# A one-core decode kernel: its first load cut into 16 and 112 rows, and the last output chunks put into other column groups

## The chip, the cores and the metric

The kernel runs on 1 core of one Trainium2 chip. The metric is the device time of one execution in microseconds. Three runs of the kernel before gave 746.25, 746.13 and 745.9, the median is 746.13.

## The reference

One token `x` of 576 features is normalised, and two branches are added to it.

```python
xn = _layernorm(x, axis=-1)
return x + _A_ref(xn, ...) + _B_ref(xn, ...)
# A: q = xn @ wq, 32 heads of 128; scores over 8192 cached keys, scale 128 ** -0.5
#    p = softmax(scores); o = p @ v_cache; out = o.reshape(1, 1, 4096) @ wo
# B: gate = xn @ W_gate, up = xn @ W_up (4608 wide); h = gate * (gate > 0) * up; out = h @ W_down
```

Everything is float32. For each of 32 heads the cache holds 8192 x 128 keys and as many values, 4.2 MB each; with the weights the program reads 319 MB, each byte once, and writes 576 numbers.

## The kernel before

**Loads.** Three buffers in SBUF, `slot0` to `slot2`, of 128 rows (partitions) x 16384 floats, are filled in turn by DMAs that SyncE (SP) issues in one written order. The helper `load` (its DMA is line 159) issues one DMA for one buffer, or for a part of its columns. The first three need no wait: `wq` into slot 0 (128 rows of 64 KB, the query weights), `wqt` into slot 1 (the rest of the query weights and a first part of gate and up weights), `wg` into slot 2 (more of them). Then come 32 loads `kv[n]`, each with the values of head n - 1 in the first half of the columns and the keys of head n in the second (the first one has gate and up weights in place of values), `vw`, and nine loads of `wod`, the rows of `wo` and `W_down` in one order, 576 columns for each chunk of 128 rows. A load waits until its buffer has been read, so up to two wait in the DMA queue behind the one that moves. The DMAs of an issuing engine go through one queue, and 16 DMA engines work on it.

**Work.** Layer norm is done by VectorE (DVE) and ScalarE (ACT) on one row while `wq` is on its way. TensorE (PE) then computes `q` with 36 matmuls into the bank `bq`, of which the first waits for `wq` and the thirty-third for `wqt`. Each head's keys are multiplied with the broadcast query on DVE (line 287) and summed (line 292), ACT takes the exponentials (line 306), and PE sums the values with them (helper `values`; all plain matmuls have line 216).

**End.** There are 68 output chunks, f = 0 to 67: 32 heads of `wo` and 36 parts of `W_down`. Each adds one row of 576 numbers as two matmuls of 288 columns (j = 0, 1). A float32 matmul is two instructions in the trace, so a chunk is four MATMULs. Output row r selects the column group of PE in which a matmul runs. Even chunks go to rows 0 and 32 of the bank `acc` (called here the lower column groups), odd ones to rows 64 and 96 of the bank `ac2` (the upper ones); the last `LAST` = 4 chunks, 64 to 67, all go to the lower groups. When chunk 63 is done (mark "odd"), DVE adds the odd chunks' sum to `x2`, in which `x` already lies in rows 64 and 96 (line 412, mark "y"); PE adds the result to `acc` with two matmuls (four MATMULs) that pick these rows with columns of the identity. These stand in PE's order after chunk 65 and ahead of chunks 66 and 67:

```python
if f == end - 2:
    for j in range(2):
        mm(("y",) if j == 0 else (), None, acc[32 * j:32 * j + 1, :N2],
           ident[:, 64 + 32 * j:65 + 32 * j], x2, False, False)
```

After chunk 67, DVE and ACT each copy one half of the result out of `acc` (lines 413 and 414), and SP writes it out (line 182). `OUT` sets how the chunks are grouped into loads: 9 of them come with `vw`, then one load of 28, loads of 9, 7, 5, 4 and 3, and one load each for chunks 65, 66 and 67. Their matmuls wait for "o" of their own load.

Each engine runs its list in the written order. Waits are on semaphores; each DMA here has one, which reaches its full count when all 16 DMA engines are done.

Of the kernel before, what the change touches and what calls it, by code (L numbers as in the profile page):

```python
# [9 lines left out]
P = 128  # L10
# [13 lines left out]

OUT = ((9,), (28,), (9, 7, 5, 4, 3), (1, 1, 1))

LAST = 4

UNITS = (28, 32, 16, 5)

# [6 lines left out]
class Program:  # L37
# [19 lines left out]
    def add(self, engine, f, waits=(), mark=None, on=None, by=1):  # L57
        to = None
        if mark is not None:
            to = on or engine  # L60
            self.sem(to)
            self.counts[to] += by
            assert mark not in self.marks, mark
            self.marks[mark] = (to, self.counts[to])
        self.lists[engine].append((f, tuple(waits), to, by))
# [41 lines left out]
def build(nc, x, kv, vw, wq, wqt, wg, wod, out):  # L107
    pr = Program(nc)
    add = pr.add

    def sb(name, shape):
        return nc.alloc_sbuf_tensor(name, list(shape), F32).ap()

    def bank(name):
        return nc.alloc_psum_tensor(name, [P, 512], F32).ap()

    slots = [sb(f"slot{i}", [P, W]) for i in range(3)]
# [13 lines left out]
    xz = sb("xz", [P, 4, 37])  # L131
# [15 lines left out]
    bq, bb, bm, bo, bt, acc, ac2, bx = [bank(f"bank{i}") for i in range(8)]  # L147
# [9 lines left out]
    def load(name, k, src, waits, on, start=0):  # L157
        dst = slots[k % 3][:, start:start + src.shape[-1]]
        add("sync", lambda e: e.dma_start(dst, src), waits, name, on=on, by=16)  # L159

    def tile(n):
        return slots[(n + 3) % 3]

    load("wq", 0, wq, (), "dwq")
    load("g0", 1, wqt, (), "dg0")
    load("g1", 2, wg, (), "dg1")
    load(("t", 0), 3, kv[0], ("pq",), "dt0")
# [6 lines left out]
    f = OUT[0][0]  # L174
# [40 lines left out]
    def mm(waits, mark, o, lhsT, rhs, start, stop):  # L215
        add("tensor", lambda e: e.matmul(o, lhsT, rhs, start=start, stop=stop), waits, mark)  # L216
# [5 lines left out]
    for k in range(36):  # L222
        if k < 32:
            r, a, j = k // 16, k // 4 % 4, k % 4
            mm(("wq", "xz") if k == 0 else (), None, bq[32 * j:32 * j + 32, :], xz[:, a, 5 - r:37 - r],
               slots[0][:, a * 4096 + (4 * r + j) * 512:][:, :512], k < 4, False)
        else:
            j = k - 32
            mm(("g0", "xt") if k == 32 else (), "pq" if k == 35 else None, bq[32 * j:32 * j + 32, :], xt[:, 5:37],
               slots[1][:, j * 512:(j + 1) * 512], False, True)  # L230
# [105 lines left out]
    for n in range(1, H):  # L336
        k, i = (n - 1) // G, (n - 1) % G
# [52 lines left out]
    f, end = 0, H + FC  # L390
# [3 lines left out]
    for k, loads in enumerate(OUT):  # L394
        t = tile(H)[:, SK + UNITS[3] * 512:] if k == 0 else slots[(H + 3 + k) % 3]
        i = 0
        for n in loads:
            for m in range(n):
                waits = (("o", f),) if m == 0 and k else ()
                waits += needs.get(f, ())  # L400
                odd = f % 2 and f < end - LAST
                for j in range(2):
                    r = 64 * odd + 32 * j
                    mark = {OUT[0][0] - 1: ("first", f), end - LAST - 1: "odd", end - 1: "even"}.get(f) if j else None
                    mm(waits if j == 0 else (), mark, (ac2 if odd else acc)[r:r + 1, :N2], order[f], t[:, i * D + j * N2:][:, :N2],
                       f < 2, f in (end - LAST - 1, end - 1))
                f += 1
                i += 1
                if f == end - 2:
                    for j in range(2):  # L410
                        mm(("y",) if j == 0 else (), None, acc[32 * j:32 * j + 1, :N2], ident[:, 64 + 32 * j:65 + 32 * j], x2, False, False)
    add("vector", lambda e: e.tensor_add(x2[64:P, :], ac2[64:P, :N2], x2[64:P, :]), ("odd", "x2"), "y")  # L412
# [62 lines left out]
```

## Time and profile before

| what | value |
|---|---|
| median of three runs | 746.13 us |
| the profiled execution | 745.72 us, of which 744.2 us lie between its first and last instruction (the span) |
| PE, DVE, ACT, POOL busy | 41%, 78%, 5%, 0% of the span |
| queue q1 (SP's loads) | 319.17 MB, 99.3% of the time of 16 DMA engines |
| mean granted TensorE clock | 0.661 of full speed |

The span leaves 1.5 us of the profiled execution outside. The profiled execution is 0.41 us below the median. Busy shares are means over the whole span; the start (no data yet) and the end (no data left to load) have other limits than the middle.

### The profile page before, as it was taken

Reading aid. Unit: us, or ns where it says so; the run is one execution under the profiler, and the core shown is the slowest. Engines: PE = TensorE matmul, PEld = TensorE weight load, DVE = VectorE, ACT = ScalarE, POOL = GpSimd, SP = SyncE. Lnnn points to the kernel's source line nnn. Section 1 sums busy time; section 2 is a strip of 40 time slices with the busy share of each in tenths; the row PEclk is TensorE's granted clock in tenths of the full one; section 3 lists DMA queues with packets and bytes.
Section 4 is the critical chain, followed back from the end, with each engine's and each line's share of the span. In section 5 each row is a group of like instructions: output and inputs, shape, how many; then the busy total and the mean of one; then the engine's idle time right before and its main releaser. Section 6 shows DMA issues by size and latency. Waiting matters only on the chain.

```text
span 744.2 us, 4062 instructions
## 1 busy us (share of the span) xinstructions
PE 302.0 (41%) x1752; PEld 87.4 (12%) x1752; DVE 577.2 (78%) x177; ACT 36.5 (5%) x114; POOL 2.1 (0%) x10
## 2 busy tenths in 40 slices
PE   1454413343253343352343344334324325334677
PEld 1111100010010010010010011001001001001122
DVE  2000189999989999989999998998998998999610
ACT  1000001010010010010000001001001000000000
POOL 1000000000000000000000000000000000000000
PEclk9967755767655565556556656655565565565789
DMA  9999999999999999999999999999999999999997
GB/s 395 451 420 426 445 451 402 440 451 405 444 447 413 444 437 444 416 440 444 412 440 447 412 440 444 412 447 437 437 423 440 444 412 437 451 409 438 432 414 319
DMA packets 6498, 319.30 MB, mean 429 GB/s; under 512 B 724, under 2 KB 726, under 8 KB 1240
## 3 DMA queue, kind: packets, MB, share of 16 engines
q1 hardware_dynamic: 6482, 319.17, 99.3%
q8 instruction: 6, 0.10, 0.1%
q14 instruction: 4, 0.03, 0.0%
q10 hardware_dynamic: 6, 0.00, 0.0%
HBM read 319.16 MB, written 0.00 MB: 429 GB/s over the span
## 4 chain that ended last, share of the span: by engine, by line
DMA 45%; DVE 22%; issue 20%; PE 11%; ACT 1%; SPq 0%; DVEq 0%; ACTq 0%
DMA slot<-in_kv 35%; DVE slot L287 12%; PE bank L216 11%; DVE s L292 9%; DMA slot<-in_wqt 5%; DMA slot<-in_wod 5%; ACT row L310 1%; ACT pzs L306 0%; DVE nb L296 0%; DVE mr L293 0%; SPq L159 0%; DVE os L300 0%; DVE row L413 0%; DVE rl L299 0%; DVEq L101 0%
## 5 line engine op out<-in xcount | busy, mean ns | idle before, releaser
L287 DVE TENSOR_TENSOR slot<-slot,bank 128x8192 f32<-128x8192 f32 x32 | 277.9, 8686 | 82.3 <-PE bank L216 65.8
L292 DVE TENSOR_REDUCE s<-slot 128x64 f32<-128x8192 f32 x32 | 277.6, 8676 | 0.0
L216 PE MATMUL bank<-slot,pzs 128*12 128x512 f32 x1024 | 184.7, 888 | 201.9 <-ACT pzs L306 201.9
L216 PEld LDWEIGHTS bank<-slot,pzs 128*12 128x12 f32 x1024 | 35.4, 123 | 332.5 <-issue 332.3
L216 PE MATMUL bank<-slot,xz 128*32 128x512 f32 x208 | 36.7, 732 | 32.1 <-DMA slot<-in_wq 12.8
L216 PE MATMUL bank<-ident,mr 128*128 128x128 f32 x64 | 17.6, 360 | 73.8 <-DVE mr L293 73.7
L216 PE MATMUL bank<-l,ones 128*128 128x3 f32 (+1 forms) x22 | 6.3, 354 | 98.2 <-ACT pzs L306 98.2
L306 ACT ACTIVATE pzs<-s,nb 128x64 f32<-128x64 f32 x32 | 11.1, 348 | 457.3 <-issue 419.4
L237 DVE TENSOR_SCALAR row<-bank 128x512 f32<-128x512 f32 x1 | 0.7, 692 | 33.8 <-PE bank L216 33.8
L216 PEld LDWEIGHTS bank<-ident,mr 128*128 128x128 f32 x64 | 10.7, 210 | 95.6 <-DVE mr L293 95.4
L412 DVE TENSOR_TENSOR x<-bank,x 64x288 f32<-64x288 f32 x1 | 0.5, 460 | 26.9 <-PE bank L216 26.9
L216 PEld LDWEIGHTS bank<-l,ones 128*128 128x128 f32 x22 | 5.3, 299 | 101.5 <-ACT pzs L306 100.7
L274 ACT ACTIVATE dq<-ident,qs 128x128 f32<-128x128 f32 x32 | 10.7, 392 | 130.7 <-PE bank L216 90.6
L216 PE MATMUL bank<-dq,ones 128*128 128x384 f32 (+1 forms) x24 | 15.3, 737 | 0.0
L216 PEld LDWEIGHTS bank<-slot,xz 128*32 128x32 f32 x208 | 8.5, 131 | 57.8 <-issue 23.6
L216 PE MATMUL bank<-sel,row 128*128 128x3 f32 (+1 forms) x88 | 11.6, 254 | 7.9 <-ACT row L310 7.9
L216 PE MATMUL bank<-slot,os 128*1 128x288 f32 x128 | 11.3, 500 | 4.7 <-DMA slot<-in_wod 4.7
L216 PEld LDWEIGHTS bank<-sel,row 128*128 128x128 f32 x88 | 10.6, 191 | 17.5 <-ACT row L310 17.5
L216 PE MATMUL bank<-slot,hh 128*1 128x288 f32 x144 | 11.2, 406 | 3.2 <-DMA slot<-in_wod 3.2
L216 PE MATMUL bank<-slot,xt 128*32 128x512 f32 x26 | 6.8, 1021 | 10.8 <-DMA slot<-in_wqt 10.8
L310 ACT COPY row<-bank 128x512 f32<-128x512 f32 x11 | 6.4, 585 | 77.2 <-PE bank L216 77.2
L296 DVE TENSOR_REDUCE nb<-bank 128x1 f32<-128x128 f32 x32 | 9.1, 284 | 0.6 <-PE bank L216 0.6
(52 smaller groups left out, 54.3 us busy)
## 6 DMA issues: line engine op xcount, KB each, us to landing
slot<-in_wod SPq DMA_DIRECT2D x1, 8064.0 KB, 39.3
slot<-in_vw SPq DMA_DIRECT2D x1, 7968.0 KB, 39.6
slot<-in_wod SPq DMA_DIRECT2D x1, 2592.0 KB, 25.9
slot<-in_wod SPq DMA_DIRECT2D x1, 2016.0 KB, 30.4
slot<-in_wod SPq DMA_DIRECT2D x1, 1440.0 KB, 33.3
slot<-in_wod SPq DMA_DIRECT2D x1, 1152.0 KB, 35.6
slot<-in_wod SPq DMA_DIRECT2D x1, 864.0 KB, 36.9
slot<-in_wod SPq DMA_DIRECT2D x3, 288.0 KB, 25.0
```

The lines of the kernel that those rows point to most:

```text
L216: add("tensor", lambda e: e.matmul(o, lhsT, rhs, start=start, stop=stop), waits, mark)
L237: add("vector", lambda e: e.tensor_scalar_mul(row, bq, SCALE), ("pq", "n7"), "qr")
L274: add("scalar", lambda e, m=m, h=h: e.activation(dq[:, m, :], ident, AF.Copy, scale=qs[:, h:h + 1]), (free,) if m == 0 else (), ("dq", k) ...
L287: add("vector", lambda e: e.tensor_mul(k3, k3, qb[:, m, None, :].to_broadcast([P, C, DH])), waits, ("mul", h))
L292: add("vector", lambda e: e.reduce_sum(s, k3, axis=AX.X), (("mul", h),), ("sum", h))
L296: add("vector", lambda e: e.tensor_reduce(nb[h % 2], pm, axis=AX.X, op=ALU.max, negate=True), (("pm", h),), ("nb", h))
L306: add("scalar", lambda e: e.activation(pz[:, i, :, 4 * G - 4:4 * G], s2[h % 2].rearrange("p (c b) -> p c b", b=4), AF.Exp, bias=nb[h % 2], ...
L310: add("scalar", lambda e: e.copy(row, bo), (("V", h),) + ((("ot", k - 1),) if k else ("pqt",)), ("oc", k), on="oc", by=STEP)
L412: add("vector", lambda e: e.tensor_add(x2[64:P, :], ac2[64:P, :N2], x2[64:P, :]), ("odd", "x2"), "y")
```

## The change

It has two parts that don't touch each other. The load of `wq` becomes two DMAs on the same queue, rows 0 to 15 and rows 16 to 127, each with its own semaphore; the first matmul of `q` waits for both. `LAST` becomes 2, so chunk 64 stays in the lower and chunk 65 goes to the upper column groups; the mark "odd" moves from chunk 63 to chunk 65, and the four MATMULs that add `x2` move from after chunk 65 to after chunk 66.

```diff
-LAST = 4
+LAST = 2
...
-    load("wq", 0, wq, (), "dwq")
+
+    add("sync", lambda e: e.dma_start(slots[0][:16, :], wq[:16]), (), "wq0", on="dwq0", by=16)
+    add("sync", lambda e: e.dma_start(slots[0][16:P, :], wq[16:]), (), "wq", on="dwq", by=16)
     load("g0", 1, wqt, (), "dg0")
...
-            mm(("wq", "xz") if k == 0 else (), None, bq[32 * j:32 * j + 32, :], xz[:, a, 5 - r:37 - r],
+            mm(("wq0", "wq", "xz") if k == 0 else (), None, bq[32 * j:32 * j + 32, :], xz[:, a, 5 - r:37 - r],
...
-                if f == end - 2:
+                if f == end - 1:
```

## The prediction

> **What bounds the kernel now.** I read the page first, for which engine has no idle time, then the DMA queue over the middle of the run, then the first and the last microseconds instruction by instruction.
>
> ```profile
> PE 302.0 (41%) x1752; PEld 87.4 (12%) x1752; DVE 577.2 (78%) x177; ACT 36.5 (5%) x114; POOL 2.1 (0%) x10
> DMA  9999999999999999999999999999999999999997
> q1 hardware_dynamic: 6482, 319.17, 99.3%
> DMA 45%; DVE 22%; issue 20%; PE 11%; ACT 1%; SPq 0%; DVEq 0%; ACTq 0%
> ```
>
> No engine is near its limit: DVE is busy 78%, PE 41%. The queue of loads is: the packets of q1 fill 99.3% of the time of 16 DMA engines, and every slice of the span but the last is full. The chain of waits names DMA, DVE and PE, but a chain also passes through work that merely runs beside the loads. The view by windows settles it for the middle (columns: window, its length, busy time of PE, PEld, DVE, ACT, POOL, clock, DMA share, GB/s):
>
> ```profile
> 20.00:730.00 710.00, 289.99 (x1624) 81.81 (x1628) 571.48 (x160) 32.48 (x108) 0.00 (x0) 0.64 1.00 432
> ```
>
> From 20 to 730 us the DMA share is 1.00. So a microsecond that the queue loses or gains anywhere ahead of 730 us moves the end by one, unless a load is issued too late. The issues and their times to landing (us, last number) say that this has slack:
>
> ```profile
> slot<-in_wq SPq DMA_DIRECT2D x1, 21.7
> slot<-in_wqt SPq DMA_DIRECT2D x1, 40.6
> slot<-in_wg SPq DMA_DIRECT2D x1, 60.8
> slot<-in_kv SPq DMA_DIRECT2D x32, 39.3
> ```
>
> A `kv` load is issued 39.3 us before it lands, while one load takes about 19.3 us (next fence), so there is a whole load queued ahead of it.
>
> **The change part by part: the start.** The timeline of the first stretch:
>
> ```profile
> 0.73 0.52 ACTq L194 DMA_DIRECT2D row<-in_x  x1
> 0.74 0.40 SPq L159 DMA_DIRECT2D slot<-in_wq  x1
> 1.20 0.42 SPq L159 DMA_DIRECT2D slot<-in_wqt  x1
> 1.66 0.42 SPq L159 DMA_DIRECT2D slot<-in_wg  x1
> 22.53 8.53 PE L216 MATMUL bank<-slot,xz 128*32 128x512 f32 x64 [12.77 <-DMA slot<-in_wq]
> 41.85 1.94 PE L216 MATMUL bank<-slot,xt 128*32 128x512 f32 x8 [10.79 <-DMA slot<-in_wqt]
> 43.85 28.06 SPq L159 DMA_DIRECT2D slot<-in_kv  x3
> ```
>
> Three loads are issued within 1.4 us, yet their readers start at 22.53 and 41.85 us, 19.3 us apart: the queue serves whole loads one after the other. That is the point on which I rest: 16 rows in a DMA of their own are moved first, with nothing of the other 112 rows beside them to fill engines that they leave slow.
>
> How the 16 DMA engines begin, by slices of 0.05 us from 1 to 3 us, and by windows (same columns as above):
>
> ```profile
> GB/s 0 0 0 0 0 0 0 0 0 0 0 0 0 46 0 5243 1311 3932 2621 2621 0 0 0 0 2621 1311 0 0 1311 0 0 0 0 0 0 0 0 0 0 0
> q1 hardware_dynamic: 16, 1.05, 152.1%
> 1.70:2.50 0.80, 0.00 (x0) 0.00 (x0) 0.44 (x2) 0.12 (x1) 0.27 (x3) 1.00 3.80 1311
> 2.50:4.70 2.20, 0.00 (x0) 0.00 (x0) 0.96 (x3) 2.17 (x4) 0.00 (x0) 1.00 0.00 0
> 4.70:5.30 0.60, 0.00 (x0) 0.00 (x0) 0.00 (x0) 0.60 (x1) 0.00 (x0) 1.00 4.03 1748
> ```
>
> Bytes are counted where a packet starts. 16 packets, 1.05 MB, start between 1.75 and 2.45 us: 64 KB each, one row for each engine. None starts from 2.50 to 4.70, the next 16 do so by 5.30. So a load is 8 turns of one row per engine, 19.3 / 8 = 2.4 us a turn, 27 GB/s per engine.
>
> *The earlier start.* The first DMA now has 16 rows to be set up instead of 128. The nearest row is the one-row load of `x`: issued at 0.73, its 2.2 KB packet is the 46 in the slice from 1.65, 0.92 us later. From the issue at 0.74 that would be 1.66, against first packets from 1.75 to 2.45 now. So between 0.1 and 0.8 us are to be gained on an engine; a few of the 16 start late, most by 2.0, so I take -0.3. Below it -0.8; above it +0.3, for one more completion per engine and a set-up that gains nothing.
>
> *The second DMA.* SP issues one more, some 0.46 us by the step from 0.74 to 1.20. `wq`'s rest then goes at 1.20, `wqt` at 1.66, `wg` at 2.12. The first rows keep the engines busy to about 4.7 us, so nothing runs dry; the next issue on SP is `kv[0]` at 43.85, which waits for PE. Cost 0. POOL's and ACT's queues are not passed. The extra wait ("wq0") stands ahead of the first matmul of `q`; all of PE is behind it, but it was already waiting 12.77 us for `wq`, which lands later than `wq0`. Cost 0 while that holds.
>
> *What 16 neighbouring rows cost.* In every load of this trace the 16 engines work on all 128 rows. No row shows them on rows 0 to 15 only. Fast end: they take one turn as now, 2.4 us, cost 0. Slow end: each set of rows takes bytes no faster than it does in a full load, where rows 0 to 15 take theirs in the whole 19.3 us; cost 19.3 - 2.4 = +16.9. Neither row is nearer, since both are of full loads: one shows what an engine can send, the other what these rows took. I take the middle, (2.4 + 19.3) / 2 = 10.9 us, hence +8.4, and keep 0 and +16.9 for the range. Cover: none, by the DMA share of 1.00.
>
> The Trainium skill, "SBUF — State Buffer", section "Door 1: The DMA port swizzle", says that a DMA's rate goes by how many of 16 ports its partitions reach, that partitions 0 to 15 reach four, and that 1 MiB to them was measured at 104 GB/s. By it this DMA would take an estimated 1.05 MB / 104 GB/s = 10.1 us instead of 2.4, and the sum would be 753.5. No row here shows such a DMA.
>
> *The 112 rows.* Seven turns per engine. Fast end: 7 x 2.4 = 16.9 us, as in a full load, cost 0. Slow end: two engines meet at each turn and halve, cost +16.9. The nearest row is the full load, which differs by 16 rows of 128: I take 0.
>
> **The change: the end.** PE's and DVE's timeline, and the three single-chunk loads (65, 66, 67) with their least, median and longest time to landing:
>
> ```profile
> 739.38 1.62 PE L216 MATMUL bank<-slot,hh 128*1 128x288 f32 x16 [0.98 <-DMA slot<-in_wod]
> 740.11 0.46 DVE L412 TENSOR_TENSOR x<-bank,x 64x288 f32<-64x288 f32 x1 [26.93 <-PE bank L216]
> 740.62 0.30 PEld L216 LDWEIGHTS bank<-x,ident 128*1 128x1 f32 x4 [0.19 <-DVE x L412]
> 740.83 0.66 PE L216 MATMUL bank<-x,ident 128*1 128x288 f32 x4
> 741.31 1.14 PE L216 MATMUL bank<-slot,hh 128*1 128x288 f32 x8
> 742.50 0.45 DVE L413 COPY row<-bank 1x288 f32<-1x288 f32 x1 [1.93 <-PE bank L216]
> L216 PE MATMUL bank<-x,ident x4: 406/406/406, 740.8 to 741.1; 128*1 128x288 f32 x4
> L159 SPq DMA_DIRECT2D slot<-in_wod x3: 328/418/430, 715.3 to 716.2; - x3
> DMA to landing us min/median/max: 24.7/25.0/25.3
> ```
>
> A MATMUL of 288 columns lasts 0.41 us (406 ns). The 8 of chunks 66 and 67, all in the lower groups, take 1.14: (1.14 - 0.41) / 3 = 0.24 us from step to step, two steps a chunk. The 16 of chunks 62 to 65 take 1.62, (1.62 - 0.41) / 0.24 = 5 intervals, six steps: 62 and 63 share two, 64 and 65 take two each. Chunks 65, 66 and 67 land at 715.3 + 24.7 = 740.0, about 740.7, and 716.2 + 25.3 = 741.5.
>
> Before, from 739.38 on: 62/63, 64, 65, y, 66, 67, twelve steps without a gap, 739.38 + 11 x 0.243 + 0.41 = 742.46. DVE's add (740.11 to 740.57) lay wholly under 64 and 65. After: 62/63 at 739.38 and 739.62; 64 at 739.86 and 740.10; 65, released at 740.0, beside 64's second step at 740.10 and then at 740.34. It ends at 740.75. DVE starts 0.08 later, as it did after chunk 63 (739.62 + 0.41 = 740.03, start 740.11): 740.83 to 741.29. The cover for it is now chunk 66 alone (landed 740.7, steps 740.78 and 741.02, over by 741.27). The matmuls of y, queued ahead of chunk 67, wait to 741.34 and 741.58; chunk 67 follows at 741.82 and 742.07, end 742.47. Chunk 67 landed at 741.5 and waits for y in both kernels. So two steps saved in the column groups (-0.49) come back as a wait for DVE: 0.0. If 65 lands one step earlier against PE it is -0.24, one later +0.24.
>
> **Sum**, on the profiled execution: 745.72 - 0.3 + 8.4 + 0 + 0.0 = 753.8. The median lies 0.41 higher, so 754.2.
>
> **The rivals.**
>
> *Not slower: the 16 rows take one turn.* Then the split does what it says and the stream begins earlier: 746.13 - 0.3 + 0.0 = 745.8, with -0.8 and -0.24 at best 745.1, with +0.3 and +0.24 at worst 746.7. For it: an engine sends 27 GB/s to a row today, and its share is the same with 16 rows. Against it: nothing shows that neighbouring rows accept 16 engines at once. It decides from 1.2 us on: if the 16 rows take less than 2.4 + 0.3 + 1.5 = 4.2 us, the result is within 0.2% (1.5 us, about what a measurement of this kernel can tell from no change).
>
> *The 112 rows are uneven as well.* Rows 16 to 127 no longer start where the engines' shares of a full load start. At half of the slow end, +8.4, on top of the forecast: 762.6. For it: one engine late is enough, since a load's semaphore waits for all. Against it: 112 is seven full turns of 16.
>
> *Faster by more than 1.5 us.* The best ends together are -0.8 - 0.24 = -1.0, 745.1; so it needs something that no row shows.
>
> **How the numbers follow.** Forecast 45%; the uneven 112 rows 10%; not slower 42%; clearly faster 3%. I put the two sides close together, as the fence of the first packets leaves the 16 rows open between 2.4 and 19.3 us, and only 1.5 of those 16.9 us belong to "no change"; but the fast end is one plain case and the slow side a spread. Slower by over 0.2%: 45 + 10 = 55%; within: 42%; faster: 3%. The range goes from 745.1, the good end of the rival, to 763.0 (746.13 + 16.9), and leaves out parts of the last two. The forecast's own range is 749 to 763.
>
> **What would show it.** Slow 16 rows: few bytes start between 5 and 12 us, q's first matmul moves from 22.53 to about 30.6 us, the `wqt` readers from 41.85 to about 49.9, and all later steps of 19.3 us stay. One turn: q's first matmul is at about 22.2. Uneven 112 rows: the first matmul later than 33. At the end: the `x2` add (now L414) starts 0.8 us after chunk 65 lands in place of beside its matmuls, PE has a gap of some 0.07 us between chunk 66 and y, and the span from PE's start on chunks 62 to 64 to the copies stays 3.1 us. The prediction is wrong if the first load lands as early as before, or if the end moves by more than 0.3 us by itself.

## The result and the profile after

The changed kernel takes 767.36 us (median of 6 runs, 766.39 to 768.51) against 746.23 for the kernel before (6 runs, 745.9 to 747.5): 1.0284 times as long, 95% interval 1.027 to 1.0297. It is slower by 21.1 us; the forecast was 754.2, slower by 8, with a range up to 763.0.

The page of the changed kernel, the lines that answer to those shown of before, and the rate by slices:

```profile
PE 300.0 (39%) x1752; PEld 88.3 (12%) x1752; DVE 576.8 (75%) x177; ACT 36.5 (5%) x114; POOL 2.1 (0%) x10
DMA  9999999999999999999999999999999999999997
GB/s 165 267 380 432 438 438 407 433 438 438 421 438 431 435 438 435 428 425 438 438 438 431 428 438 431 431 438 435 431 425 438 438 438 425 431 438 433 430 412 304
q1 hardware_dynamic: 6498, 319.17, 99.2%
DVE 48%; DMA 40%; PE 7%; issue 4%; another core or an unknown queue 1%; ACT 0%; SPq 0%; DVEq 0%; ACTq 0%
```

The busy times are the same within some 2 us, and the DMA share hardly moved: 99.2% and a row of nines, in a run that lost 21 us in its loads. The share counts the time that packets took, and a packet that crawls counts as busy. The loss is in the line below it: 165, 267 and 380 GB/s in the first three slices (19.1 us each), 407 and more after that, but for the last slice (304; 319 before). A DMA share has to be read beside its GB/s. The shares of the chain moved (DVE from 22% to 48%, issue from 20% to 4%, DMA from 45% to 40%) although DVE's busy time did not change (577.2 and 576.8 us): the chain passes through work that runs beside the loads.

The first stretch of the changed kernel, then its windows from 3 to 9.5 and from 12 to 43 us, and the same windows of the kernel before (columns: window, length, PE busy, clock, DMA share, GB/s):

```profile
0.74 0.39 SPq L165 DMA_DIRECT2D slot<-in_wq  x1
1.19 0.40 SPq L166 DMA_DIRECT2D slot<-in_wq  x1
1.64 0.42 SPq L159 DMA_DIRECT2D slot<-in_wqt  x1
44.50 9.23 PE L218 MATMUL bank<-slot,xz 128*32 128x512 f32 x64 [34.73 <-DMA slot<-in_wq]
63.75 1.94 PE L218 MATMUL bank<-slot,xt 128*32 128x512 f32 x8 [10.02 <-DMA slot<-in_wqt]
```
```profile
3.00:9.50 6.50, 2.45 (x12) 1.00 0.00 0
12.00:43.00 31.00, 0.00 (x0) 1.00 0.91 233
```
```profile
3.00:9.50 6.50, 2.45 (x12) 1.00 0.75 323
12.00:43.00 31.00, 9.68 (x72) 0.88 1.01 438
```

q's first matmul starts at 44.50 us in place of 22.53, 22.0 us later; the readers of `wqt` at 63.75 in place of 41.85, 21.9 later and again 19.3 us after the first load. So the whole loss is in the first load, and it is there by 44.5 us. It has two parts. From 3 to 9.5 us no new packet starts at all: the first 16 are still under way (a window counts a packet, its time and its bytes, where it starts, so its DMA share of 0.00 does not mean idle engines). Then the 112 rows move at 233 GB/s, about half the 438 of before. The first DMA (line 165) took 12.5 us from issue to landing, the second (line 166) 43.2:

```profile
DMA to landing us min/median/max: 12.5/12.5/12.5
```
```profile
DMA to landing us min/median/max: 43.2/43.2/43.2
```

They land at 0.74 + 12.5 = 13.2 and 1.19 + 43.2 = 44.4 us. So the 112 rows had 31.2 us, where seven turns of 2.4 are 16.9.

The end of the changed kernel, then the last part of the chain of work that ended last:

```profile
760.95 2.09 PE L218 MATMUL bank<-slot,hh 128*1 128x288 f32 x20 [0.96 <-DMA slot<-in_wod]
762.35 0.46 DVE L414 TENSOR_TENSOR x<-bank,x 64x288 f32<-64x288 f32 x1 [26.47 <-PE bank L218]
762.86 0.66 PE L218 MATMUL bank<-x,ident 128*1 128x288 f32 x4
763.35 0.66 PE L218 MATMUL bank<-slot,hh 128*1 128x288 f32 x4
764.05 0.45 DVE L415 COPY row<-bank 1x288 f32<-1x288 f32 x1 [1.24 <-PE bank L218]
```
```profile
738.41 23.93 DMA slot<-in_wod
762.34 0.04 issue
762.38 1.65 PE bank L218 x12
```

From PE's start on chunks 62 to 64 to the copies it is 764.05 - 760.95 = 3.10 us; before, 742.50 - 739.38 = 3.12. The steps saved in the column groups came back as a wait for the load of chunk 66. The chain passes through its landing at 762.34, and the 12 MATMULs behind it are chunk 66, y and chunk 67. Chunk 66 starts at 762.38, its two steps of 0.24 us are over at 762.86, and y starts there without a gap. DVE was done a little earlier (line 414 ends at 762.81).

### The profile page after: what moved, and what is told of

Its sections match the earlier page's. It is cut to its first block, busy times and chain, and to the rows that moved or that the text cites. A ratio compares the mean times of both kernels' runs of the same rounds, so it can differ in the third digit from the quotient of the medians.

```text
span 765.7 us, 4063 instructions
## 1 busy us (share of the span) xinstructions
PE 300.0 (39%) x1752; PEld 88.3 (12%) x1752; DVE 576.8 (75%) x177; ACT 36.5 (5%) x114; POOL 2.1 (0%) x10
## 3 DMA queue, kind: packets, MB, share of 16 engines
q1 hardware_dynamic: 6498, 319.17, 99.2%
## 4 chain that ended last, share of the span: by engine, by line
DVE 48%; DMA 40%; PE 7%; issue 4%; another core or an unknown queue 1%; ACT 0%; SPq 0%; DVEq 0%; ACTq 0%
DMA slot<-in_kv 26%; DVE slot L289 24%; DVE s L294 23%; PE bank L218 7%; DMA slot<-in_wq 6%; DMA slot<-in_vw 5%; DMA slot<-in_wod 3%; DVE mr L295 1%; DVE nb L298 1%; ACT row L312 0%; DVE os L302 0%; DVEq L101 0%; DVE rl L301 0%; ACT pzs L308 0%
```

## The experiments

Theory "rows": how fast the 16 DMA engines fill a buffer depends on which rows they are on together; a DMA whose rows don't lie evenly over all 128 goes at a part of the rate. Its rivals: a second DMA costs by itself; the number of rows costs (few, or no power of two); the end of the kernel has a part in the loss. ("The page on SBUF ports" in the expectations is the page of the Trainium skill that the prediction cites; a "group of rows" there is the rows behind one of its 16 ports.) Kernels with an interval were timed beside the kernel before. The others are one execution each; the kernel before gave 745.66 to 747.74 in these series, so single times are read to some 2 us.

**One part of the change at a time.**

```diff
 e1: -LAST = 2 / if f == end - 1      +LAST = 4 / if f == end - 2      (the changed kernel, with the end of before)
 e2: -LAST = 4 / if f == end - 2      +LAST = 2 / if f == end - 1      (the kernel before, with the new end)
```

> Only the split of the first load (16 and 112 rows); the end as before. If the split carries the loss: 767 to 768 us, q's first matmul at about 44.5 us in place of 22.5. If the end has a part in it: under 766.

> Only the end is changed (last two chunks in the lower column groups, the odd sum added ahead of the last chunk alone); the first load is whole. By the steps of the prediction: 746.2, within 0.3 us of before, PE's stretch from the chunks 62 to 64 to the copies 3.1 us. Rival: the end costs or gains more than 0.5 us.

The split alone: 766.8 us, a little under the 767 to 768 expected, ratio 1.027 (1.0255 to 1.0286), q's first matmul at 44.56. The end alone: 745.92 against 746.06, ratio 0.9996 (0.9987 to 1.0005). The end of e2:

```profile
739.55 2.08 PE L216 MATMUL bank<-slot,hh 128*1 128x288 f32 x20 [0.97 <-DMA slot<-in_wod]
740.96 0.46 DVE L412 TENSOR_TENSOR x<-bank,x 64x288 f32<-64x288 f32 x1 [27.69 <-PE bank L216]
741.47 0.65 PE L216 MATMUL bank<-x,ident 128*1 128x288 f32 x4
742.66 0.45 DVE L413 COPY row<-bank 1x288 f32<-1x288 f32 x1 [1.24 <-PE bank L216]
```

742.66 - 739.55 = 3.11. The split carries all of the loss within the noise, and the end is worth nothing in either direction.

**Is it the second DMA, the count, or the rows?** In e3 to e10 the first load is cut in other ways; all else is the kernel before. Each piece has its own semaphore, and q's first matmul waits for all.

```diff
-    load("wq", 0, wq, (), "dwq")
+    # e3: rows :64 and 64:            e4: all rows, columns :2048 and 2048:
+    # e5: rows 0::2 and 1::2          e6: rows i::8, i = 0 to 7
+    # e7: rows 16*i:16*i+16, i = 0 to 7   e8: rows :112 and 112:
+    # e9: rows :32 and 32:            e10: rows i::4, i = 0 to 3
+    add("sync", lambda e: e.dma_start(slots[0][:64, :], wq[:64]), (), "wq0", on="dwq0", by=16)   # e3
+    add("sync", lambda e: e.dma_start(slots[0][64:P, :], wq[64:]), (), "wq1", on="dwq1", by=16)
```

> The first load in two DMAs of 64 rows each (0 to 63, 64 to 127); the end as before. Theory rows (each group of rows takes only its own share of the rate; by the page on SBUF ports 64 neighbouring rows reach half of 16 ports): each half takes twice its time, the first load lands some 19 us later, 765 us. Rival count (112 is no power of two, or is 7 rows an engine, and that is slow): no loss, 746. Rival two DMAs (the second one's set-up or completion costs): the same as with 16 and 112 rows, 767.

> The first load in two DMAs of all 128 rows, columns 0 to 2047 and 2048 to 16383; the end as before. Theory rows: no loss, 746 within 0.5 us, as all rows are filled at once by both. Rival two DMAs: well above 746, up to 767.

Two DMAs of all rows (e4): 745.93 us, ratio 0.9993 (0.9984 to 1.0002). Two DMAs of 64 rows each (e3): 767.38, ratio 1.0279 (1.0264 to 1.0295). The first matmul on `wq` in e4 and in e3:

```profile
22.59 9.29 PE L217 MATMUL bank<-slot,xz 128*32 128x512 f32 x64 [12.81 <-DMA slot<-in_wq]
```
```profile
43.98 6.36 PE L217 MATMUL bank<-slot,xz 128*32 128x512 f32 x40 [34.22 <-DMA slot<-in_wq]
```

A second DMA costs nothing. 64 is a power of two, and two DMAs of 64 rows lose as much as 112 and 16. Over eight turns e3 loses 43.98 - 22.53 = 21.45 us, so a turn of 2.4 takes 5.1. That rules out that a second DMA costs by itself, and that a power of two is enough to be fast. It does not show whether 112 rows are slow by their number as well.

> The first load in two DMAs of 64 rows each, the even rows and the odd rows. Both reach every group of rows, as a whole load does. If a DMA's rate goes by the rows that it reaches in all: no loss, 746 us, q's first matmul at about 22.5. If it goes by the rows that the 16 engines are on at the same moment, each engine having its own run of the DMA's rows: two engines meet in each group as with rows 0 to 63, about 765 to 767, first matmul near 43.5.

> The first load in eight DMAs of 16 rows each, every eighth row (0, 8, .. 120; then 1, 9, ..). By the page on SBUF ports such rows reach 8 of 16 ports, two rows each: twice the time for each DMA, the first one lands at about 7 us, q's first matmul at about 41 to 44, 765 to 767 us. If 16 rows in one DMA cost what they cost because they are few: 9 to 10 us for each of the eight, over 800.

> The first load in eight DMAs of 16 neighbouring rows each (0 to 15, 16 to 31, ..). Theory rows: each takes four times a turn of 2.4 us, eight of them 77 us in place of 19.3, q's first matmul at about 80, the end at 804. If only the first one is slow (a start-up matter): 753 to 755. If eight DMAs of one row an engine cost the same wherever their rows lie: the same as with every eighth row.

Even and odd rows (e5): 746.09. Eight DMAs of every eighth row (e6): 767.34. Eight DMAs of 16 neighbours (e7): 801.05. The first matmul on `wq` in e5, e6 and e7, and the landing of e7's first DMA:

```profile
22.90 8.36 PE L217 MATMUL bank<-slot,xz 128*32 128x512 f32 x64 [13.09 <-DMA slot<-in_wq]
```
```profile
44.42 9.92 PE L223 MATMUL bank<-slot,xz 128*32 128x512 f32 x64 [34.61 <-DMA slot<-in_wq]
```
```profile
78.12 9.92 PE L223 MATMUL bank<-slot,xz 128*32 128x512 f32 x64 [68.18 <-DMA slot<-in_wq]
```
```profile
DMA to landing us min/median/max: 12.0/12.0/12.0
```

64 rows to a DMA cost 21 us when they are neighbours (e3) and nothing when they are every second row (e5). 16 rows to a DMA take twice a turn when they are eight apart (e6: 44.42 - 22.53 = 21.9 us more for eight, so 5.1 us each) and four times when they are neighbours: e7's last seven DMAs take (78.12 - 12.7) / 7 = 9.3 us each, 112 GB/s. So for 16 and 64 rows it is which rows they are and not how many, and it isn't a matter of the start: all eight pay. Of my two variants for e5, the one in which each engine has its own run of the DMA's rows falls.

> The first load as 112 rows (0 to 111) and then 16 rows (112 to 127). Theory rows, with seven neighbouring rows to each engine: the 112 rows take about 26 to 32 us in place of 16.9, the 16 rows about 7 us more than their turn, 760 to 768 us in all. If 112 rows are slow only behind the 16 (the engines thrown out of step by them): the 112 land at about 19 us and the loss is that of the 16 alone, 753 to 755.

> The first load as 32 rows (0 to 31) and then 96 rows (32 to 127), six rows an engine. The 32 rows reach 8 groups of rows of 16: two turns at twice the time, landing at about 12 us (4 to 5 us lost). For the 96: if the long second part of 16 and 112 rows was slow because seven rows an engine don't fit the groups, 96 rows have at best 8 turns (their fullest groups have 8 rows), about 19.3 us, so q's first matmul at about 31 to 32 and 755 to 757 us. If any second part that isn't half or all of the rows goes at half the rate: 96 rows take about 29 us, first matmul at about 41, 765 us.

> The first load in four DMAs of 32 rows each, every fourth row: two rows for each engine, and each group of rows gets two. If a small DMA is at full rate when its rows lie evenly over all groups: the first lands at about 7.5 us, q's first matmul at 22.5 to 23, 746 to 747 us. If few rows in a DMA cost in themselves: later than 30.

112 rows first (e8): 766.93 us. 32 and 96 rows (e9): 766.36. Four DMAs of every fourth row (e10): 746.28. The landing of e8's first DMA, the windows, the first matmul and the first DMA's landing of e9, the landing of e10's first DMA and its first matmul:

```profile
DMA to landing us min/median/max: 34.9/34.9/34.9
```
```profile
3.00:9.50 6.50, 2.31 (x11) 1.00 0.79 161
12.00:43.00 31.00, 0.00 (x0) 1.00 0.94 211
43.17 8.35 PE L217 MATMUL bank<-slot,xz 128*32 128x512 f32 x64 [33.27 <-DMA slot<-in_wq]
DMA to landing us min/median/max: 12.4/12.4/12.4
```
```profile
DMA to landing us min/median/max: 7.6/7.6/7.6
23.02 8.47 PE L219 MATMUL bank<-slot,xz 128*32 128x512 f32 x64 [13.24 <-DMA slot<-in_wq]
```

112 rows are slow with nothing ahead of them: 34.9 us to landing, where the whole load of 128 rows takes 21.7; the time is in the 760 to 768 expected. So it is not the 16 rows ahead that throw the others out of step. For e9 I had expected 755 to 757 from the theory that seven rows an engine don't fit; it was 766, with the 96 rows at 211 GB/s. That explanation falls; the time is nearer to the 765 of the other one, half the rate. The 32 neighbours landed after 12.4 us, as expected. e10 shows that a DMA of only 32 rows runs at the full rate when its rows are spread: 7.6 us to landing for two turns, and q's first matmul at 23.02.

In sum, the pieces that kept the full rate are all rows, every second row and every fourth. Every piece of neighbours (16, 32, 64, 96 and 112 rows), and every eighth row, went at about half the rate or less, whatever came before it. "Evenly over all 128" is thus not the whole rule: every eighth row lies evenly too, and e6 came out at half, as expected. No run moved 96 or 112 rows otherwise than as neighbours.

## Why the prediction was wrong

**What bounds the kernel** was right: a microsecond lost by the queue in the first load moved the end by one. 22.0 us at q's first matmul arrive as 764.05 - 742.50 = 21.6 at the last copies.

**The step that failed is "The 112 rows": "I take 0".** They cost 31.2 - 16.9 = 14.3 us in the changed kernel, close to the slow end of 16.9 that stood beside it, "two engines meet at each turn and halve". I chose the full load as the nearest row since it differs by only 16 rows of 128. e8 and e9 show that nearness in number says nothing: 112 and 96 neighbours go at about half the rate. The rival of uneven 112 rows named the right term, but at 10%, at half its price, and for reasons that the runs don't bear out. One was that rows 16 to 127 start elsewhere than a full load; e8's 112 rows start at row 0 and are as slow. The other was that one late engine is enough; the packets of e9 are slow on all engines alike. There, from 16 to 28 us in slices of 0.3:

```profile
GB/s 218 874 1748 655 0 0 0 0 0 0 0 0 0 0 0 0 0 218 874 1748 655 0 0 0 0 0 0 0 0 0 0 0 0 0 874 1748 437 437 0 0
DMA packets 48, 3.15 MB, mean 262 GB/s; under 512 B 0, under 2 KB 0, under 8 KB 0
```

The 48 packets start in three bursts of 16, as many as there are engines. Each burst is over in 1.2 us, and the bursts are some 5 us apart in place of 2.4. What makes such rows slow is open. How the rows of a DMA are dealt to the engines does not show in these traces, and my one explanation for it, too many rows in the fullest groups, was refuted by e9. Nor is it shown that the places of the rows are to blame here: 112 and 96 are also no powers of two, and that rival stands untested.

**What 16 neighbouring rows cost** was right in kind and not far off in size: 10.9 us taken, +8.4. As the middle of two far bounds, 0 and +16.9, the size was in part luck. e4's first DMA moves as many bytes over all 128 rows, 4.8 us from issue to landing:

```profile
slot<-in_wq SPq DMA_DIRECT2D x1, 1024.0 KB, 4.8
```

The 16 rows landed after 12.5, which is +7.7. e7 gives 9.3 - 2.4 = +6.9 for each later one. The Trainium skill's figure in "SBUF — State Buffer" (section "Door 1: The DMA port swizzle"), 104 GB/s for 1 MiB to partitions 0 to 15, agrees with the 112 GB/s of e7, and its half rate for partitions 0 to 63 with e3's 5.1 us a turn. Its rule by the ports that the partitions reach stops there: 112 rows reach all 16 of its ports and still went at half the rate.

**The earlier start** did not come. First packets of the changed kernel, from 1 to 3 us in slices of 0.05:

```profile
GB/s 0 0 0 0 0 0 0 0 0 0 0 0 0 46 0 0 5243 1311 1311 0 0 0 0 1311 0 1311 0 2621 1311 2621 1311 0 0 0 1311 1311 0 0 0 0
```

They start from 1.80 to 2.75, before from 1.75 to 2.45. The moment of the first packet does not go by the number of rows, so the -0.3 is 0.

**The second DMA** and **the extra wait** cost 0, as e4 shows, which has both.

**The end** was right in its times: y 1.91 us after the start on chunks 62 to 64 (forecast 741.34 - 739.38 = 1.96), 3.10 us to the copies (forecast 3.1), 0.0 in all (e2). Its reason was not: the forecast gap of some 0.07 us between chunk 66 and y did not come, and PE waited for chunk 66's load, not for DVE. e2's chain passes through that landing as well, at 740.92. The prediction's own steps say the same when they are read again: of the two steps it saved, one is lost because chunk 65 lands late, some 0.20 us because chunk 66 does (740.78 in place of 740.34 + 0.24), and only 0.07 to DVE (741.34 in place of 741.27).

With the measured terms, 7.7 + 14.3 + 0 + 0 = 22.0, the delay of q's first matmul, against 21.1 between the medians. **The range** failed with the sum: its upper end of 763.0 let one of the two DMAs be at its slow end and not both. Both were slow in one run, so the two ends had to be added.

The Trainium skill, "DMA: Bandwidth & Descriptors", section "Rules for kernel authors", says of two transfers to disjoint halves of the partitions not to bother and to use one of 128 partitions, since they run one after the other on the same engines. e3 agrees and goes further: here the two halves cost 21 us more than the one load.

## What to carry to other kernels

As far as these loads of 64 KB rows show, keep every large load on all 128 rows, and cut it by columns (e4) or by every second or fourth row (e5, e10) if it must be cut; runs of neighbouring rows lost about half the rate or more, and in a kernel bound by its loads all of that is paid at the end. Read GB/s beside the DMA share, as the share stays full when packets crawl. When two terms may be slow for the same reason, add both slow ends for the range. Before steps are saved at the end of a kernel, look at when its last loads land: a freed engine only waits for them.

## What was not expected of the hardware

SP takes longer over the first issue when it is a DMA of every second, fourth or eighth row, or of 64 neighbours, than when it is one of 128, 112, 32 or 16 neighbours. The first issue of e10:

```profile
L164 SPq DMA_DIRECT2D slot<-in_wq x1: 558/558/558, 0.7 to 0.7; - x1
```

That is 0.56 us (0.56 to 0.62 in e3, e5 and e6), against 0.39 to 0.40 in the changed kernel, before, e7, e8 and e9. The first matmul is 0.4 to 0.5 us later in e5 and e10 (22.90 and 23.02 against 22.53), so the harmless cuts were not gains either. None of the versions tried is faster than the kernel before beyond the noise.
